# An S5 scan layer on Trainium2: rotating the scan's inputs in place in six chunk slots, with a new instruction order

## The chip, the cores and the metric

The kernel runs on one core of one Trainium2 chip. The time is that of one execution on the device, in microseconds (us), and less is better. Engines are named as the profile names them: PE is TensorE (PEld its weight loads), DVE is VectorE, ACT is ScalarE, POOL is GpSimd, SP is SyncE.

## The reference, cut to what matters

```python
xn = layernorm(x)                                  # x: 1 x 2048 x 1024, bfloat16
# part A: a diagonal complex recurrence over 2048 steps, 1024 states
Bu = einsum("bld,pd->blp", xn, B_bar)              # complex B_bar
for t in range(2048):
    h = Lam_bar * h + Bu[:, t, :]                  # complex Lam_bar
y = 2 * einsum("blp,dp->bld", h_all, C).real + xn * Dskip
# part B: the two tokens with the largest xn @ w_r go through a gated MLP (1024 x 3584)
return x + y + part_B
```

The kernel cuts the 2048 steps into 16 chunks of 128. The scan instruction that it uses on DVE is given a real recurrence. So within each chunk the input is turned by the angle of `Lam_bar` to the power of minus t ("turn in", TI), then two real scans run with the modulus of `Lam_bar` as decay (SC), and their result is turned back ("turn out", TO). One turn of a complex array is three DVE instructions: a product with the cosines, a product of the swapped halves (real and imaginary part exchanged) with the signed sines, and a sum.

## The kernel before

A frame is two chunks. PE computes `Bu` for a frame, one block of 128 states at a time; ACT moves it from PSUM into `u`; DVE turns `u` into `v`; the scan reads `v`. Tables `E1c` and `E1s` hold cosines and signed sines.

```python
def evac_u(f, j):                                  # ACT
    if j == 0:
        u_tiles[f] = work.tile([128, 2, PT, TF], BF16, name="u", bufs=2)
    nc.scalar.copy(out=u_tiles[f][:, :, j, :], in_=pB_tiles.pop((f, j))[:])

def v_tile(c):
    if c not in v_tiles:
        v_tiles[c] = work.tile([128, 2, PT, T + 2], BF16, name="v", bufs=2)
    return v_tiles[c]

def turn_in(c, js=ALLJ):                           # DVE
    f, cc = divmod(c, CPF)
    u = u_tiles[f][:, :, js, cc * T:(cc + 1) * T]
    v = v_tile(c)
    m = work.tile([128, 2, PT, T], BF16, name="m", tag="m")
    rot = v[:, :, js, 2:]
    nc.vector.tensor_tensor(out=rot, in0=u, in1=both(E1c, js), op=ALU.mult)
    nc.vector.tensor_tensor(out=m[:, :, js, :], in0=u[:, ::-1], in1=E1s[:, :, js, :], op=ALU.mult)
    nc.vector.tensor_add(out=rot, in0=rot, in1=m[:, :, js, :])
...
def turn_out(c, js=ALLJ):                          # DVE; cut
    nc.vector.tensor_tensor(out=rot, in0=g, in1=E2c[:, :, js, :], op=ALU.mult)
    nc.vector.tensor_tensor(out=m[:, :, js, :], in0=g[:, ::-1], in1=both(E2s, js), op=ALU.mult)
    nc.vector.tensor_add(out=rot, in0=rot, in1=m[:, :, js, :])
```

`u[:, ::-1]` is the swap. There is one scratch tile `m` for all turns. Chunks 0 to 3 are turned in two halves, the last chunk in three parts, all others whole: 22 turns in and 22 turns out. The order of all instructions comes from a small planner: every task has a duration, its dependencies and a priority, and a table `ADJUST` of searched numbers shifts the priorities.

Of the kernel before, what the change touches and what calls it, by code (L numbers as in the profile page):

```python
# [9 lines left out]
ACT = mybir.ActivationFunctionType  # L10
ALU = mybir.AluOpType
# [6 lines left out]
T = 128  # L18
TF = 256
# [6 lines left out]
    ('x', 4): -5.4, ('x', 6): 45.2, ('x', 8): 30.6, ('x', 9): 9.9, ('x', 10): 81.6, ('x', 11): 60.3, ('x', 12): 21.2,  # L26
    ('B', 5, 0): 1.8, ('B', 5, 1): 1.6, ('B', 6, 0): 2.8, ('B', 6, 1): 38.2, ('B', 7, 0): 42.4, ('B', 7, 1): 15.8,
    ('C', 0, 0): 21.6, ('C', 0, 1): 20.8, ('C', 1, 0): 2.1, ('C', 1, 1): -2.7,
    ('sum', 5): 26.9, ('sum', 10): 38.6, ('sum', 12): 204.6, ('sum', 15): 15.9,
    ('nmr1', 6): 56.1, ('nmr1', 7): 212.5, ('nmr1', 9): 214.1, ('nmr1', 10): 74.8, ('nmr1', 11): 61.1,  # L30
    ('sq', 7): -48.4,
    ('xnT', 7): -3.8434110173345237, ('xnT', 8): 2.330756354758774, ('xnT', 9): -1.9681120886767554,
    ('xnT', 11): -0.20571159998656965, ('xnT', 12): 35.53687818863374, ('xnT', 13): -5.08116404784938,
    ('xnT', 14): -1.6392153513862842, ('xnT', 15): -42.082253982643586,
    ('nmr', 8): -107.7, ('nmr', 10): -98.5,
    ('rstd', 9): 5.9,
    ('sin',): -3.6,
    ('ts', 1, 0): 172.7, ('ts', 1, 1): 108.6,
    ('E2n', 0): 1.2, ('E2n', 1): -21.3,
    ('Bu', 1, 0): -7.9, ('Bu', 1, 1): -5.9, ('Bu', 1, 2): -31.7, ('Bu', 1, 3): -0.8, ('Bu', 1, 4): -5.6,  # L40
    ('Bu', 1, 5): -10.1, ('Bu', 1, 6): -0.2, ('Bu', 4, 0): -22.1, ('Bu', 4, 1): 4.5, ('Bu', 4, 2): -2.5,
    ('Bu', 4, 3): 5.0, ('Bu', 4, 4): -6.4, ('Bu', 4, 5): -2.2, ('Bu', 4, 7): -0.6, ('Bu', 5, 0): 20.6,
    ('Bu', 5, 1): -49.1, ('Bu', 5, 2): 20.5, ('Bu', 5, 3): -0.3, ('Bu', 5, 4): -8.4, ('Bu', 5, 5): -0.7,
    ('Bu', 5, 6): -15.7, ('Bu', 5, 7): -6.8, ('Bu', 6, 0): 51.2, ('Bu', 6, 1): -9.1, ('Bu', 6, 2): 1.9,
    ('Bu', 6, 3): -7.5, ('Bu', 6, 4): -12.6, ('Bu', 6, 5): 2.0, ('Bu', 6, 6): -22.7, ('Bu', 6, 7): 1.9,
    ('Bu', 7, 0): 290.1, ('Bu', 7, 1): -0.4, ('Bu', 7, 2): -0.1, ('Bu', 7, 3): 11.1, ('Bu', 7, 4): -9.4,
    ('Bu', 7, 5): 9.3, ('Bu', 7, 6): 29.7, ('Bu', 7, 7): -1.4,
    ('u', 2, 0): -11.8, ('u', 2, 1): -26.4, ('u', 2, 2): 34.9, ('u', 2, 3): 2.1, ('u', 2, 5): -4.0,
    ('u', 2, 6): -4.9, ('u', 3, 1): -16.1, ('u', 3, 2): -44.1, ('u', 3, 4): -44.6, ('u', 3, 7): 1.0,
    ('u', 4, 0): 15.6, ('u', 4, 1): 44.8, ('u', 4, 2): 42.7, ('u', 4, 4): -3.8, ('u', 4, 5): 11.0, ('u', 4, 6): 7.7,  # L50
    ('u', 4, 7): 17.3,
    ('TI', 0, 0): -19.7, ('TI', 0, 4): -3.0, ('TI', 1, 0): -4.9, ('TI', 1, 4): -7.9, ('TI', 8, 0): 62.9,
    ('TI', 9, 0): 73.1, ('TI', 11, 0): -11.8, ('TI', 13, 0): 30.7, ('TI', 14, 0): -38.5, ('TI', 15, 0): 346.6,
    ('TI', 15, 4): -34.3, ('TI', 15, 6): 673.0,
    ('cw', 0, 0): 12.6, ('cw', 0, 4): 12.6, ('cw', 1, 0): 12.5, ('cw', 1, 4): 13.3,
    ('SC', 1, 0, 0): 22.2, ('SC', 1, 0, 1): 75.7, ('SC', 1, 4, 0): 23.4, ('SC', 1, 4, 1): 3.3,
    ('SC', 3, 0, 0): 112.8, ('SC', 3, 0, 1): 6.5, ('SC', 3, 4, 0): 7.0, ('SC', 3, 4, 1): 10.7, ('SC', 4, 0, 0): -0.1,
    ('SC', 4, 0, 1): -11.3, ('SC', 12, 0, 0): 18.6, ('SC', 12, 0, 1): 3.0, ('SC', 15, 0, 0): 25.5,
    ('SC', 15, 0, 1): 22.6, ('SC', 15, 4, 0): 41.8, ('SC', 15, 4, 1): 22.5, ('SC', 15, 6, 0): 45.9,
    ('SC', 15, 6, 1): 7.2,  # L60
    ('TO', 2, 0): 11.0, ('TO', 2, 4): -7.4, ('TO', 4, 0): -50.9, ('TO', 12, 0): 34.1, ('TO', 13, 0): -130.1,
    ('xr', 0): -17.4, ('xr', 3): 13.0, ('xr', 4): 21.4, ('xr', 5): 34.6, ('xr', 6): 49.5, ('xr', 7): 49.6,
    ('xr', 8): 55.2, ('xr', 9): 56.6, ('xr', 10): 84.8, ('xr', 11): 69.2, ('xr', 12): 93.2, ('xr', 13): 87.9,
    ('xr', 14): 189.0, ('xr', 15): 224.2,
    ('Y', 2, 0): 40.8, ('Y', 2, 1): 0.2, ('Y', 2, 2): 3.9, ('Y', 2, 3): -17.0, ('Y', 3, 0): -23.2, ('Y', 3, 1): 0.3,
    ('Y', 3, 2): 11.7, ('Y', 3, 3): 3.3, ('Y', 6, 0): -4.6, ('Y', 6, 1): 1.7, ('Y', 6, 2): 7.9, ('Y', 6, 3): -8.6,
    ('Y', 10, 0): 18.7, ('Y', 10, 1): 54.9, ('Y', 10, 2): 30.2, ('Y', 10, 3): 5.8, ('Y', 11, 0): 4.6,
    ('Y', 11, 1): 4.6, ('Y', 11, 2): -11.7, ('Y', 11, 3): -0.2, ('Y', 12, 0): 48.7, ('Y', 12, 1): -1.0,
    ('Y', 12, 2): 15.0, ('Y', 12, 3): 18.1,
    ('ADD', 4, 0): 66.6, ('ADD', 4, 1): 8.9,  # L70
    ('xm', 9): 32.0, ('xm', 10): 23.8,
    ('w', 3): -25.8, ('w', 16): 88.5, ('w', 18): 165.2, ('w', 20): 219.3, ('w', 22): 156.0, ('w', 23): 216.5,
    ('w', 24): 167.0, ('w', 25): 222.5, ('w', 26): 167.6, ('w', 27): 179.1, ('w', 28): 168.4, ('w', 29): 222.5,
    ('w', 30): 231.4, ('w', 31): 166.6, ('w', 32): 210.4, ('w', 33): 166.1, ('w', 34): 187.3, ('w', 35): 257.2,
    ('w', 36): 190.5, ('w', 37): 217.1, ('w', 38): 243.4, ('w', 39): 196.1, ('w', 40): 198.1, ('w', 41): 246.5,
    ('mm', 12): 30.3,
    ('gT', 1): 64.4,
# [88 lines left out]
def kernel(  # L166
# [24 lines left out]
    NF = L // TF  # L191
    CPF = TF // 128
# [81 lines left out]
    for tag, n in (("xt", 4), ("xn", 2), ("xnT", NF - 2), ("pT", 1), ("pB", 3), ("pY", 3), ("u", 2), ("v", 2), ("gf", 2),  # L274
                   ("gb", 2), ("hT", 3), ("xr", 1), ("xa", 1), ("ot", 2), ("w", 2)):
        pl.ring(tag, n)
# [47 lines left out]
    xnT_tiles = {}  # L324
# [66 lines left out]

    def xnT_part(c):
        f, cc = divmod(c, CPF)
        if f not in xnT_tiles:
            xnT_tiles[f] = work.tile([128, DT, TF], BF16, name="xnT", bufs=NF - 2)
        return xnT_tiles[f][:, :, cc * T:(cc + 1) * T]
# [43 lines left out]
    for c in range(NCH):  # L440
        ln = c - 30
        xn_out = ("Tpe", c) if c < PE_T else ("T", c)
        xnT_take = ("xnT", c // CPF, [("Y", (c // CPF) * CPF + 1, 2)])
# [29 lines left out]
        if c < PE_T:  # L473
            if c == 0:
                add(("TpeA",), "PE", 0.24, lambda: transpose_half(0), [("applyA",)], key=ln - 10, takes=[("pT", ("T", c), [("xnT", c)])])
                add(("Tpe", c), "PE", 0.24, lambda: transpose_half(1), [("apply", c), ("TpeA",)], key=ln - 10, takes=[("pY", ("T", c), [("xnT0",)])])
                add(("xnT0",), "DVE", 0.42, evac_T0, [("Tpe", c)], key=-36, takes=[xnT_take])
            else:
                add(("Tpe", c), "PE", 0.48, lambda c=c: transpose_pe(c), [("apply", c)], key=ln - 10,
                    takes=[("pY" if c < 4 and c % 2 else "pT", ("T", c), [("xnT", c)])])  # L480
            add(("xnT", c), "ACT", 0.92 if c else 0.55, lambda c=c: evac_T(c), [("Tpe", c) if c else ("TpeA",)], key=-41 + c if c < 2 else ln - 10, takes=[xnT_take])
        else:
            add(("T", c), "SP", 1.35, lambda c=c: transpose_dma(c), [("apply", c)], key=-60 + c, takes=[xnT_take], mb=0.28, lag=0.7)
# [156 lines left out]
    def stage_Bu(f, j, ts_=slice(0, TF)):  # L640
# [3 lines left out]
        for ri in range(2):  # L644
            for k in range(DT):
                nc.tensor.matmul(out=pB[:, ri, ts_], lhsT=BT[ri][j][:, k, :], rhs=xnT_tiles[f][:, k, ts_],  # L646
                                 start=(k == 0), stop=(k == DT - 1))

    def evac_u(f, j):
        if j == 0:  # L650
            u_tiles[f] = work.tile([128, 2, PT, TF], BF16, name="u", bufs=2)
        nc.scalar.copy(out=u_tiles[f][:, :, j, :], in_=pB_tiles.pop((f, j))[:])  # L652

    HALVES = ((0, 0), (0, 1), (1, 0), (1, 1), (1, 2))
# [4 lines left out]
    for f in range(NF):  # L659
        for j in range(PT):  # L660
            hs = (f, j) in HALVES
            if hs:
                add(("Bh", f, j), "PE", 0.93, lambda f=f, j=j: stage_Bu(f, j, slice(0, T)), [("B", j, 0), ("B", j, 1), ("xnT", f * CPF)] + ([] if f else [("xnT0",)]),
                    key=2 * f - 3 + j / 8, takes=[("pB", (f, j), [("u", f, j)])])
            add(("Bu", f, j), "PE", 0.93 if hs else 1.75, lambda f=f, j=j, hs=hs: stage_Bu(f, j, slice(T if hs else 0, TF)),
                [("B", j, 0), ("B", j, 1)] + [("xnT", f * CPF + cc) for cc in range(CPF)] + ([("Bu", f, j - 1)] if j else [])
                + ([("Bh", f, j)] if hs else []), key=2 * f - 3 + j / 8, takes=[("pB", (f, j), [("u", f, j)])])
# [498 lines left out]
```

## Time and profile before

| | before |
|---|---|
| time, median of 3 runs | 265.95 us |
| span of the profiled run | 264.4 us |
| PE busy | 256.5 us, 97% |
| DVE busy | 251.5 us, 95% |
| ACT busy | 158.9 us, 60% |
| one whole product or sum of a turn (128x2048 bf16) | 1.22 us |
| idle DVE from its first statistics to its last turn | 2.53 us |

PE and DVE are both nearly always busy. The last row is the sum of the gaps of 0.05 us and more between the end of one DVE instruction and the start of the next. (The prediction left out gaps under 0.04 us and got 2.9.)

A row of the timeline has a start, a duration, engine, line, operation, output and inputs. This is the turn in of one whole chunk in the kernel before; the columns are start, duration, engine, line, operation, output and inputs:

```profile
69.64 1.22 DVE L697 TENSOR_TENSOR v<-u,E1c 128x2048 bf16<-128x2048 bf16 x1
70.78 1.22 DVE L698 TENSOR_TENSOR m<-u,E1s 128x2048 bf16<-128x2048 bf16 x1
72.04 1.22 DVE L699 TENSOR_TENSOR v<-v,m 128x2048 bf16<-128x2048 bf16 x1
73.19 0.68 DVE L759 TENSOR_TENSOR hT<-gb,E2c 128x1024 bf16<-128x1024 bf16 x1
```

The first product would end at 70.86, yet the second one starts at 70.78, 0.08 us earlier: the two overlap, and the distance is 1.14 us. The second product ends at 72.00, and the sum starts at 72.04, after it: it needs what the second product writes, and the distance is 1.26 us. The instruction behind the sum overlaps again (1.15). So an instruction that depends on the one directly ahead costs about 0.12 us more of DVE's time than one that doesn't, and no duration shows it. I call such a start **held**.

### The profile page before, as it was taken

What the parts mean: (1) busy time and instruction counts of PE and PEld (TensorE: products, weight loads), DVE (VectorE), ACT (ScalarE), POOL (GpSimd) and SP (SyncE); (2) the same over time, 40 slices, a digit from 0 to 9 for tenths busy, and PEclk for the clock granted to TensorE, in tenths of its full rate; (3) what the DMA queues carried; (4) which work ended last, traced back from release to release, by engine and by line L of the source; (5) the groups of instructions that cost most, each with busy time, mean ns of one, the idle gap of its engine ahead of it and who ended that gap; (6) DMA issues with size and microseconds to landing.
All of it is one profiled execution on the core that took longest, in us unless ns stands there. A gap on an engine that the chain in (4) does not pass through costs nothing.

```text
span 264.4 us, 5522 instructions
## 1 busy us (share of the span) xinstructions
PE 256.5 (97%) x2207; PEld 173.2 (66%) x2227; DVE 251.5 (95%) x334; ACT 158.9 (60%) x281; POOL 83.6 (32%) x126
## 2 busy tenths in 40 slices
PE   7799999999999999999999999999999999999994
PEld 7799988774688457456756586455864776644461
DVE  6999999999999999999999999999998999999992
ACT  3799999959699999996524447034551533145110
POOL 4221303563545440731040217115260409011100
PEclk9999999999999999999999999999999999999999
DMA  8999999998541125416111197588967884770411
GB/s 180 188 175 218 171 235 229 248 271 293 153 137 57 47 60 165 138 40 183 58 62 60 35 360 237 187 266 287 296 235 253 289 272 175 269 288 20 117 46 40
DMA packets 66165, 46.51 MB, mean 176 GB/s; under 512 B 45844, under 2 KB 52122, under 8 KB 66140
## 3 DMA queue, kind: packets, MB, share of 16 engines
q1 hardware_dynamic: 65788, 45.82, 63.4%
q8 instruction: 17, 0.28, 0.5%
q0 software_dynamic: 144, 0.27, 0.3%
q10 hardware_dynamic: 208, 0.07, 0.1%
q14 instruction: 8, 0.07, 0.1%
HBM read 30.94 MB, written 4.20 MB: 133 GB/s over the span
## 4 chain that ended last, share of the span: by engine, by line
PE 61%; DVE 28%; issue 3%; SPq 2%; ACT 2%; DMA 2%; DVEq 0%
PE pB L646 34%; PE pY L849 20%; DVE gf L718 9%; DVE ot L863 3%; PE pG L1048 3%; DVE hT L759 3%; DVE m L760 3%; DVE v L699 2%; DVE v L697 2%; DVE m L698 2%; DMA BT<-in_A_B_im_dram 2%; DVE gb L711 2%; SPq L286 2%; PE pD L1088 1%; PE pY L842 1%
## 5 line engine op out<-in xcount | busy, mean ns | idle before, releaser
L646 PE MATMUL pB<-xnT,BT 128*128 128x256 bf16 (+1 forms) x1104 | 117.5, 265 | 1.1 <-DMA BT<-in_A_B_im_dram 1.1
L849 PE MATMUL pY<-CT,hT 128*128 128x512 bf16 (+1 forms) x508 | 114.8, 372 | 1.7 <-issue 0.5
L646 PEld LDWEIGHTS <-BT 128*128 128x128 bf16 x1104 | 99.7, 98 | 16.2 <-issue 3.2
L849 PEld LDWEIGHTS <-hT 128*128 128x128 bf16 x528 | 49.1, 98 | 52.6 <-issue 3.2
L734 POOL TENSOR_TENSOR cw<-gf,tL 128x16 f32<-128x16 f32 (+1 forms) x38 | 35.0, 924 | 136.1 <-DVE gf L718 135.2
L718 DVE TENSOR_TENSOR_SCAN gf<-R,v 128x1040 f32<-128x1040 f32 (+1 forms) x38 | 69.0, 1851 | 0.2
L652 ACT CAST u<-pB 128x512 bf16<-128x512 f32 x64 | 36.5, 580 | 34.8 <-PE pB L646 34.7
L724 ACT CAST gb<-gf 128x1024 bf16<-128x1024 f32 (+1 forms) x38 | 32.4, 862 | 24.6 <-DVE gf L718 24.5
L810 ACT ACTIVATE xa<-xr,nmr_all,rstd_all 128x1024 f32<-128x1024 bf16 x12 | 14.9, 1239 | 21.9 <-DMA xr<-in_A_x_dram 8.1
L699 DVE TENSOR_TENSOR v<-v,m 128x2048 bf16<-128x2048 bf16 (+2 forms) x22 | 20.6, 938 | 0.8
L761 DVE TENSOR_TENSOR hT<-hT,m 128x2048 bf16<-128x2048 bf16 (+2 forms) x22 | 20.5, 934 | 0.8
L759 DVE TENSOR_TENSOR hT<-gb,E2c 128x2048 bf16<-128x2048 bf16 (+2 forms) x22 | 20.5, 930 | 0.2
L697 DVE TENSOR_TENSOR v<-u,E1c 128x2048 bf16<-128x2048 bf16 (+2 forms) x22 | 20.4, 928 | 0.2
L760 DVE TENSOR_TENSOR m<-gb,E2s 128x2048 bf16<-128x2048 bf16 (+2 forms) x22 | 20.5, 930 | 0.0
L698 DVE TENSOR_TENSOR m<-u,E1s 128x2048 bf16<-128x2048 bf16 (+2 forms) x22 | 20.4, 930 | 0.0
L863 DVE TENSOR_TENSOR ot<-pY,xa 128x512 bf16<-128x512 f32 (+1 forms) x25 | 16.0, 656 | 2.4 <-PE pY L852 1.8
L749 POOL CAST v<-cy 128x16 bf16<-128x16 f32 (+1 forms) x19 | 14.1, 744 | 1.4
L349 ACT ACTIVATE xn<-xt,nmean_all 128x1024 bf16<-128x1024 bf16 x12 | 13.8, 1149 | 0.3
L742 POOL TENSOR_TENSOR cy<-cw 128x16 f32<-128x16 f32 (+1 forms) x19 | 12.8, 674 | 1.5
L343 ACT ACTIVATE xn<-xt 128x1024 bf16<-128x1024 bf16 x12 | 12.6, 1054 | 0.0
L374 ACT ACTIVATE xn<-xt,nmr_all,rstd_all 128x1024 bf16<-128x1024 bf16 x10 | 12.4, 1241 | 0.3
L750 POOL TENSOR_TENSOR v<-cy,v 128x16 bf16<-128x16 f32 (+1 forms) x19 | 11.1, 586 | 1.5
(153 smaller groups left out, 186.6 us busy)
## 6 DMA issues: line engine op xcount, KB each, us to landing
wt<-in_B_w_up_dram SPq DMA_DIRECT2D x14, 512.0 KB, 5.1
wt<-in_B_w_gate_dram SPq DMA_DIRECT2D x14, 512.0 KB, 3.8
wt<-in_B_w_down_dram SPq DMA_DIRECT2D x14, 512.0 KB, 3.9
xt<-in_A_x_dram SPq DMA_DIRECT2D x16, 256.0 KB, 3.1
xr<-in_A_x_dram SPq DMA_DIRECT2D x16, 256.0 KB, 2.5
out_dram<-ot SPq DMA_DIRECT2D x31, 128.0 KB, 2.6
Drow<-in_A_Dskip_dram SPq DMA_DIRECT2D x1, 256.0 KB
xnT<-xn SPq DMA_TRANSPOSE x10, 2.8
```

The source lines that it names most:

```text
L646: nc.tensor.matmul(out=pB[:, ri, ts_], lhsT=BT[ri][j][:, k, :], rhs=xnT_tiles[f][:, k, ts_], start=(k == 0), stop=(k == DT - 1))
L652: nc.scalar.copy(out=u_tiles[f][:, :, j, :], in_=pB_tiles.pop((f, j))[:])
L697: nc.vector.tensor_tensor(out=rot, in0=u, in1=both(E1c, js), op=ALU.mult)
L698: nc.vector.tensor_tensor(out=m[:, :, js, :], in0=u[:, ::-1], in1=E1s[:, :, js, :], op=ALU.mult)
L699: nc.vector.tensor_add(out=rot, in0=rot, in1=m[:, :, js, :])
L718: nc.vector.tensor_tensor_scan(out=flat(gf), data0=flat(R[:, js, :]), data1=flat(v[:, ri, js, :]), initial=0.0, op0=ALU.mult, op1=ALU.add)
L724: nc.scalar.copy(out=gb_tiles[c][:, ri, js, :], in_=gf_tiles[c, js.start, ri][:, :, 2:])
L734: nc.gpsimd.tensor_tensor(out=cw_tiles[c, js.start][:, ri, :, 0:n], in0=g.unsqueeze(1).to_broadcast([128, 2, n]), in1=tL[:, ri, :, js], op ...
L759: nc.vector.tensor_tensor(out=rot, in0=g, in1=E2c[:, :, js, :], op=ALU.mult)
L760: nc.vector.tensor_tensor(out=m[:, :, js, :], in0=g[:, ::-1], in1=both(E2s, js), op=ALU.mult)
L849: nc.tensor.matmul(out=pY[:], lhsT=h_tiles[c][:, ri, j, :], rhs=CT[ri][h][:, j, d0:d0 + w], start=first and c in SKIP_DVE and ri == rs[0] ...
L863: nc.vector.tensor_add(out=y_tiles["ot", c][:, d_], in0=y_tiles.pop(("pY", c, dh))[:], in1=y_tiles["xa", c][:, d_])
```

## The change

The intent: keep the scan's inputs in one array of six chunk slots, rotate each in place instead of copying it from `u` to `v`, and so free memory chunk by chunk; the same for the normed x in twelve slots. With the new constraints the instruction order was searched anew, and block 1 of `B` in frame 0 does its real part first for both chunks, because the imaginary part's table lands later. The core of the diff, cut:

```diff
+    u_all = work.tile([128, NSLOT, 2, PT, T + 2], BF16, name="u_all")      # NSLOT = 6
     def evac_u(f, j):
-        nc.scalar.copy(out=u_tiles[f][:, :, j, :], in_=pB_tiles.pop((f, j))[:])
+        nc.scalar.copy(out=u_all[:, u_slots(f), :, j, 2:].rearrange("p c r t -> p r c t"),
+                       in_=pB_tiles.pop((f, j))[:].rearrange("p r (c t) -> p r c t", t=T))
...
     def v_tile(c):
-        ...
+        return u_all[:, c % NSLOT]
     def turn_in(c, js=ALLJ):
-        u = u_tiles[f][:, :, js, cc * T:(cc + 1) * T]
-        rot = v[:, :, js, 2:]
-        nc.vector.tensor_tensor(out=rot, in0=u, in1=both(E1c, js), op=ALU.mult)
+        u = v_tile(c)[:, :, js, 2:]
         nc.vector.tensor_tensor(out=m[:, :, js, :], in0=u[:, ::-1], in1=E1s[:, :, js, :], op=ALU.mult)
-        nc.vector.tensor_add(out=rot, in0=rot, in1=m[:, :, js, :])
+        nc.vector.tensor_tensor(out=u, in0=u, in1=both(E1c, js), op=ALU.mult)
+        nc.vector.tensor_add(out=u, in0=u, in1=m[:, :, js, :])
...
+    RISPLIT = ((0, 1),)        # this block of B: real part of both chunks first, then the imaginary part
...
-ADJUST = { ... }               # the order of the kernel before
+ADJUST = { ... }               # searched anew
```

Of the two products the first one must read both halves of `u` before the second one overwrites them, so the product of the swapped halves now comes first.

## The prediction

> **What bounds the kernel now.** I read the page first: busy times, then the slices, then the chain that ended last. Two engines are near their limit together.
>
> ```profile
> span 264.4 us, 5522 instructions
> PE 256.5 (97%) x2207; PEld 173.2 (66%) x2227; DVE 251.5 (95%) x334; ACT 158.9 (60%) x281; POOL 83.6 (32%) x126
> ...
> PE 61%; DVE 28%; issue 3%; SPq 2%; ACT 2%; DMA 2%; DVEq 0%
> ```
>
> The chain changes between PE and DVE: PE from 13 to 59 us, DVE from 66 to 119, PE to 232, DVE to 258. So neither can be shortened alone. The second question is how much of either engine's time is waiting. I asked for the busy time from DVE's first statistics (3.4) to its last rotation (258.2), and from the first PE work that waits for B to the same end:
>
> ```profile
> core 0: us, PE busy (x) PEld busy (x) DVE busy (x) ACT busy (x) POOL busy (x), PEclk, DMA share, GB/s
> 3.40:258.20 254.80, 251.60 (x2175) 169.96 (x2193) 249.00 (x323) 157.91 (x281) 81.68 (x115) 1.00 0.66 180
> 13.10:258.00 244.90, 243.25 (x2053) 162.41 (x2073) 239.42 (x298) 152.18 (x266) 79.04 (x105) 1.00 0.64 179
> ```
>
> From 3.4 to 258.2 DVE is idle in some 5.8 us by this sum; walking DVE's timeline with gaps under 0.04 us left out, only 2.9 us remain, the rest being the small steps between instructions. PE's own idle after 13.1 is 1.65 us. These are all the waiting that a better order has to win. The lines that carry the waits:
>
> ```profile
> 13.12 0.62 PE L646 MATMUL pB<-xnT,BT 128*128 128x128 bf16 x8 [1.13 <-DMA BT<-in_A_B_im_dram]
> ...
> DVE ot L863 <- PE pY L852: 1.8, 2, 1.5
> ...
> DVE guT L1077 <- PE pU L1068: 0.7, 1, 0.7
> ...
> DVE ot L863 <- PE pY L849: 0.5, 1, 0.5
> ...
> DVE row L918 <- PE pR L914: 0.4, 1, 0.4
> ```
>
> The first is PE at the start, waiting for the second B table; the second is the tail after the last rotation, which no buffer shortens; the other three, 0.67 + 0.52 + 0.44 = 1.63 us, are DVE waiting in the middle for PE results that the order placed a little late.
>
> **What the Trainium skill says.** (1) "Perfetto Trace Analysis", Identifying the Most-Contended Engine: matmul busy share is no good measure of headroom, because matmuls are pipelined. So I checked the pace: in the chain, 16 Y matmuls of 512 columns take 3.45 us, 216 ns each, and 32 Bu matmuls of 256 take 3.49, 109 ns each. (2) "TensorE: Matmul & The Clock Gate", "Wait — 56ns, not 53.3ns?", gives columns over 2.4 GHz plus about 2.5 ns, 215.7 ns for 512 columns; the trace agrees, so PE streams at its limit and its 97% is real here. (3) "VectorE: DVE Perf Modes", Mode 2×_1P, wants 16-bit data, step ±1 and 4-byte alignment. The new slots have rows of 130 elements (260 bytes), started at element 2 (4 bytes): aligned. The old v has just this layout, and the trace shows no cost in it, as the rows below show. (4) The first-named PE page, Architectural detail, says that VectorE's queue is strict FIFO: a late rT then holds up all DVE work behind it, whatever buffers are free. The 0.44 us before the copy from pR is such a wait.
>
> ```profile
> L761 DVE TENSOR_TENSOR hT<-hT,m 128x2048 bf16<-128x2048 bf16 x11 | 13.5, 1225 | 0.4
> L699 DVE TENSOR_TENSOR v<-v,m 128x2048 bf16<-128x2048 bf16 x11 | 13.5, 1224 | 0.4
> L697 DVE TENSOR_TENSOR v<-u,E1c 128x2048 bf16<-128x2048 bf16 x11 | 13.4, 1220 | 0.1
> L652 ACT CAST u<-pB 128x512 bf16<-128x512 f32 x64 | 36.5, 580 | 34.8 <-PE pB L646 34.7
> ```
>
> **The change, part by part.**
>
> In-place rotation. u (two frames of two chunks, 16 KB a partition) and v (two chunks, 8.1 KB) become six slots of 2 x 8 x 130 x 2 bytes, 24.4 KB: the same memory. The instruction count does not change: DVE has 333 rows before and after, ACT 264, POOL 131. The three rotation multiplies and adds stay, only the product from the swapped halves comes first. L699 is already in place and takes 1224 ns against 1225 for rows without padding, so cost 0. ACT writes u in four rows of 128 instead of two of 256; I allow 0 to 50 ns on 580, times 64 = up to 3 us, on an engine busy 60% of the span: no direct cost.
>
> Buffer waits. A wait for a u or v buffer shows nowhere in the list of waits (ACT's 34.7 us before u is for PE, with pB). So freed slots remove no wait by themselves; they only allow another order: now TI of chunks 2 and 3 stands before SC of chunk 1, and frame 3's PE work could run earlier. The twelve xn slots likewise: same 24 KB, freed a chunk at a time.
>
> Start. In Bu(0,1) the two orders differ in work: instead of both parts of B on chunk 0, then on chunk 1 (32 matmuls of 128 columns), PE does the real part on both chunks (8 of 256) and then the imaginary part (8 of 256). Before, PE did 8 of 128, waited to 13.12, and still had 8 + 16 of 128 to do: 24 x 56.6 ns = 1.36 us. After, 8 x 109 ns = 0.88 remain when the same table lands. Gain 1.36 - 0.88 = **0.48 us**, if the transposes of chunks 1 and 2 stay in the waiting time, as the order has them. PE loses 16 rows of weights and 16 of matmuls in this way.
>
> The new order. To see what it does I added up the trace's durations along each engine's order (TI or TO 3.54 us for a full chunk, 1.92 for a half; a full scan 2.24, half 1.17; ADD 0.585; a frame's Bu 1.77; a quarter of Y 1.735; the skip products 0.25), anchored DVE at 3.39 and PE at its start of Bu(0,1). On the kernel before these sums meet the trace within 1 us (Y(2,0) 85.1 against 85.03; scan of chunk 4 89.4 against 88.40). For the changed order they say:
> - ADDs come later after their Y: smallest distance 1.0 us where it was 0.2 (chunk 6). The 0.52 and 0.67 us waits should go: **-1.2 us on DVE**.
> - Y of chunk 3 now stands right behind Y(2,0), at 87.2 - 0.5 = 86.7 on PE, but its rotation ends on DVE at 89.4, less the 1.0 bias 88.4: PE waits for some **1.7 us** in all at the first four chunks.
> - rT sits behind Bu(4,6), at 128.6 - 0.5 + 1.7 = 129.8; DVE gets to the copy at 128.7 - 0.8 = 127.9. DVE waits **up to 1.9 us**, where it waited 0.44.
>
> Sum for PE: -0.5 + 1.7, less about 0.6 of small waits seen now = +0.6. Sum for DVE: -1.2 + 1.9 - 0.4 = +0.3. Without the two new waits it would be -0.5 - 0.6 = -1.1 on PE and -1.6 on DVE. Each wait is a difference of two long sums with about 1 us of error, and the order was searched anew for this layout, which speaks for waits smaller than mine. I take the middle of +0.6 and about -1.6, that is **-0.55 us: 265.4**.
>
> **Rivals.**
> 1. The order wins all waits and the head start: DVE then loses 1.63 and PE 0.5 + 0.6. The end needs both, so about -1.5 us, 264.4. For it: wider ADD distances. Against: the rT sum.
> 2. The new waits are real and push PE for good, since PE has no idle time later to catch up in: +0.6 to +1.5, 266.5 to 267.4.
> 3. ACT becomes the bound between 60 and 120 us. It is busy 19.55 of 20 us from 100 to 120, holds the norm's passes and now the strided evacuations. 32 evacuations x 50 ns would add 1.6 us there, and late norm rows would delay r(14) and rT: +1 us. Against: the same elements, in rows still long.
> 4. DVE's in-place reads are slower. At 70 ns per operation and some 16 chunks that is 1.1 us straight onto the time. Against: L699's 1224 ns.
>
> **Range and chances.** A 2% gain is 5.3 us; all waits that DVE has between 3.4 and 258.2 are 2.9, and no work is removed, so faster by over 2% is all but excluded: 0.02. A loss of 5.3 us would take several rivals at once: 0.03. Range 263.7 to 267.1: rival 1 with something to spare below, rival 2 above.
>
> **What the profile will show.** DVE busy within 1.5 us of 251.5 and the rotation rows at 1.22 us (else rival 4); the u evacuation near 580 ns (else rival 3); PE's first wait for B gone or shorter; a wait of DVE for pR of about 1 to 2 us near 128; a PE wait for hT near 87 us; no more waits of ADD and guT. The prediction is wrong if DVE's work itself changes, or if a wait over 2 us appears that my sums did not see, most likely on ACT's rows.

## The result, and the profile after

| | before, same rounds | after |
|---|---|---|
| time, median | 266.1 us (265.9 to 266.69, 4 runs) | 269.04 us (268.95 to 269.77, 4 runs) |
| span of the profiled run | 264.4 us | 267.1 us |
| DVE busy | 251.5 us | 253.1 us |
| idle DVE up to its last turn | 2.53 us | 2.82 us |
| end of DVE's last turn | 258.20 us | 260.96 us |

The ratio is 1.0113, with a 95% interval of 1.0089 to 1.0137. A ratio here is always the mean time of one kernel's fast runs over that of the kernel before in the same rounds, so it is not quite the ratio of the medians quoted beside it. The changed kernel is about 3 us slower (within 2%), where the prediction had it 0.55 us faster.

The page of the kernel after, its busy times and the chain that ended last:

```profile
span 267.1 us, 5499 instructions
...
PE 256.5 (96%) x2191; PEld 172.8 (65%) x2211; DVE 253.1 (95%) x334; ACT 159.2 (60%) x281; POOL 83.0 (31%) x126
...
DVE 46%; PE 37%; ACT 7%; issue 5%; DMA 4%; SPq 0%; DVEq 0%; ACTq 0%
```

PE has the same busy time, but the chain has moved: DVE holds 46% of it instead of 28%, PE 37% instead of 61%. DVE is busy 1.6 us longer with the same 334 instructions. Which of them became slower? The groups of the turn in, and the evacuation (busy us, then mean ns of one, then idle us just before):

```profile
L718 DVE TENSOR_TENSOR u_all<-u_all,E1c 128x2048 bf16<-128x2048 bf16 x11 | 13.5, 1226 | 0.4
L719 DVE TENSOR_TENSOR u_all<-u_all,m 128x2048 bf16<-128x2048 bf16 x11 | 13.5, 1225 | 0.4
...
L717 DVE TENSOR_TENSOR m<-u_all,E1s 128x2048 bf16<-128x2048 bf16 x11 | 13.3, 1212 | 0.2
```

None of them: 1212 to 1226 ns, and 1220 to 1225 before. The durations of all 334 instructions add up to 269.0 us in both kernels. Busy time counts a stretch in which two instructions overlap only once, so the 1.6 us are overlap that was lost. The last column is a trace of the answer: two rows of a turn in have 0.4 us ahead of them, where before only the sum had (0.4, against 0.1 and 0.0 for the products). The row of the second product before, which the prediction doesn't show:

```profile
L698 DVE TENSOR_TENSOR m<-u,E1s 128x2048 bf16<-128x2048 bf16 x11 | 13.5, 1225 | 0.0
```

The timeline of one turn in shows what this means:

```profile
64.63 1.23 DVE L717 TENSOR_TENSOR m<-u_all,E1s 128x2048 bf16<-128x2048 bf16 x1
65.89 1.23 DVE L718 TENSOR_TENSOR u_all<-u_all,E1c 128x2048 bf16<-128x2048 bf16 x1
67.15 1.22 DVE L719 TENSOR_TENSOR u_all<-u_all,m 128x2048 bf16<-128x2048 bf16 x1
```

Both distances are 1.26 us. The second product now writes what the first one reads, so it is held, and it no longer overlaps the first. In the compiled program all 22 second products of a turn in wait on DVE's own semaphore for the first; before, 10 of the 22 had no wait at all and the other 12 waited for something older. So what costs goes with a wait for the instruction directly ahead; no run has the dependency without the wait, so which of the two costs is not separated.

To see what this is worth in all, I added up the distances from start to start on DVE, by kind, from the first statistics to the end of the last turn (us; gaps of 0.05 us and more are counted apart, as idle). The same sums for the experiments follow in the same table, so that it need not be shown again:

```
                      ends at   TI products   TI sum   TO products   TO sum   scans   idle
before                 258.20      39.83       19.11      39.90       18.79   72.78   2.53
after                  260.96      42.34       19.15      39.85       19.40   72.45   2.82
x1_before_inplace      260.56      42.39       19.43      39.87       19.34   72.12   2.06
x2_before_mfirst       258.30      39.77       19.43      39.90       19.36   72.19   2.34
x3_after_const         259.56      39.78       19.19      39.80       19.49   72.43   3.60
x4_after_oldorder      261.34      42.38       19.50      39.89       19.35   72.11   2.97
x5_before_split        258.79      39.83       19.21      39.84       18.83   72.77   3.22
x8_after_sep           260.58      40.76       19.23      38.68       19.42   72.79   4.87
x9_before_split_sep    259.06      39.39       19.26      38.56       18.66   73.08   5.14
y2_after_const         258.57      39.73       19.21      39.78       19.45   72.45   2.96
y4_oldorder_const      258.90      39.66       19.57      39.86       19.40   72.10   3.22
```

The two products of the turns in took 39.83 us before and 42.34 after: +2.51 us, and DVE's last turn ends 2.76 us later. Worked out from the distances of single instructions it is nearly the same: for whole chunks the median distance went from 1.14 to 1.25 us, for halves from 0.60 to 0.72, so 11 x 0.11 + 9 x 0.12 = 2.3 us, and two quarter parts besides.

The waits moved too. These are waits of the kernel after (who waited for whom: total us, times, longest):

```profile
PE pB L659 <- ACT u_all L667: 2.4, 4, 0.9
DVE hT L779 <- ACT gb L744: 2.1, 2, 1.6
...
PEld L931 <- DVE r_bf L927: 0.7, 1, 0.7
```

The second is new, and it is on DVE. Its longer part, in DVE's timeline:

```profile
116.51 4.53 DVE L738 TENSOR_TENSOR_SCAN gf<-R,u_all 128x1040 f32<-128x1040 f32 x2
122.65 1.23 DVE L779 TENSOR_TENSOR hT<-gb,E2c 128x2048 bf16<-128x2048 bf16 x1 [1.61 <-ACT gb L744]
```

Two scans run to about 121.0, and the turn out that stands right behind them in the new order needs ACT to cast their results. ACT is in the middle of a norm pass then:

```profile
120.44 1.14 ACT L360 ACTIVATE xn<-xt,nmean_all 128x1024 bf16<-128x1024 bf16 x1
...
121.59 1.03 ACT L744 CAST gb<-gf 128x1024 bf16<-128x1024 f32 x1
```

The cast starts at 121.59, and DVE stands idle for 1.61 us. With a second wait of the same kind (0.53 us at 113) this makes 2.14 us of new waiting, against the 1.63 us of old waits (for pY, pU and pR) that are gone. So idle DVE is nearly what it was, 2.82 against 2.53, and the waits don't explain the 3 us; the held starts are the candidate.

### The profile page after: what moved, and what is told of

The parts are those of the page before. It is cut to its first block, busy times and chain, and to the rows that moved or that the text cites. A ratio compares the mean times of both kernels' runs of the same rounds, so it can differ in the third digit from the quotient of the medians.

```text
span 267.1 us, 5499 instructions
## 1 busy us (share of the span) xinstructions
PE 256.5 (96%) x2191; PEld 172.8 (65%) x2211; DVE 253.1 (95%) x334; ACT 159.2 (60%) x281; POOL 83.0 (31%) x126
## 4 chain that ended last, share of the span: by engine, by line
DVE 46%; PE 37%; ACT 7%; issue 5%; DMA 4%; SPq 0%; DVEq 0%; ACTq 0%
PE pB L659 17%; PE pY L866 15%; DVE gf L738 11%; DVE u_all L718 4%; DVE m L717 4%; DVE u_all L719 3%; DVE hT L779 3%; DVE m L780 3%; DVE hT L781 3%; DMA wt<-in_B_w_up_dram 3%; PE pG L1065 3%; DVE ot L880 2%; DVE gb L731 2%; DVE st L345 2%; ACT xn L360 1%
## 5 line engine op out<-in xcount | busy, mean ns | idle before, releaser
L659 PE MATMUL pB<-xnT_all,BT 128*128 128x256 bf16 (+1 forms) x1088 | 117.5, 266 | 2.4 <-ACT u_all L667 2.4
L754 POOL TENSOR_TENSOR cw<-gf,tL 128x16 f32<-128x16 f32 (+1 forms) x38 | 35.6, 937 | 138.3 <-DVE gf L738 137.5
L738 DVE TENSOR_TENSOR_SCAN gf<-R,u_all 128x1040 f32<-128x1040 f32 (+1 forms) x38 | 69.2, 1854 | 0.1
L667 ACT CAST u_all<-pB 128x512 bf16<-128x512 f32 x64 | 36.2, 580 | 28.4 <-PE pB L659 28.3
L718 DVE TENSOR_TENSOR u_all<-u_all,E1c 128x2048 bf16<-128x2048 bf16 (+2 forms) x22 | 20.6, 935 | 0.8
L719 DVE TENSOR_TENSOR u_all<-u_all,m 128x2048 bf16<-128x2048 bf16 (+2 forms) x22 | 20.6, 934 | 0.8
L717 DVE TENSOR_TENSOR m<-u_all,E1s 128x2048 bf16<-128x2048 bf16 (+2 forms) x22 | 20.3, 922 | 0.4
L769 POOL CAST u_all<-cy 128x16 bf16<-128x16 f32 (+1 forms) x19 | 14.6, 767 | 1.2
L762 POOL TENSOR_TENSOR cy<-cw 128x16 f32<-128x16 f32 (+1 forms) x19 | 10.9, 575 | 1.5
L770 POOL TENSOR_TENSOR u_all<-cy,u_all 128x16 bf16<-128x16 f32 (+1 forms) x19 | 10.9, 572 | 1.5
```

The lines of the kernel that those rows point to most:

```text
L659: nc.tensor.matmul(out=pB[:, ri, ts_], lhsT=BT[ri][j][:, k, :], rhs=xnT_all[:, k, x0 + ts_.start:x0 + ts_.stop], start=(k == 0), stop=(k = ...
L667: nc.scalar.copy(out=u_all[:, u_slots(f), :, j, 2:].rearrange("p c r t -> p r c t"), in_=pB_tiles.pop((f, j))[:].rearrange("p r (c t) -> p ...
L718: nc.vector.tensor_tensor(out=u, in0=u, in1=both(E1c, js), op=ALU.mult)
L719: nc.vector.tensor_add(out=u, in0=u, in1=m[:, :, js, :])
L738: nc.vector.tensor_tensor_scan(out=flat(gf), data0=flat(R[:, js, :]), data1=flat(v[:, ri, js, :]), initial=0.0, op0=ALU.mult, op1=ALU.add)
L754: nc.gpsimd.tensor_tensor(out=cw_tiles[c, js.start][:, ri, :, 0:n], in0=g.unsqueeze(1).to_broadcast([128, 2, n]), in1=tL[:, ri, :, js], op ...
```

## The experiments

Eleven kernels were run in three batches, each five rounds, each batch on one chip beside the kernel before. Two theories stood against each other at the start. **Hold:** the in-place product costs some 2.5 us on DVE through held starts, whatever the order. **Order:** the newly searched order is worse on the chip than the old one, through the waits for ACT.

### The in-place turn alone, put into the kernel before

```diff
-    nc.vector.tensor_tensor(out=rot, in0=u, in1=both(E1c, js), op=ALU.mult)
     nc.vector.tensor_tensor(out=m[:, :, js, :], in0=u[:, ::-1], in1=E1s[:, :, js, :], op=ALU.mult)
-    nc.vector.tensor_add(out=rot, in0=rot, in1=m[:, :, js, :])
+    nc.vector.tensor_tensor(out=u, in0=u, in1=both(E1c, js), op=ALU.mult)
+    nc.vector.tensor_add(out=rot, in0=u, in1=m[:, :, js, :])
```

> The kernel before, its order and buffers untouched; only the first rotation's products are swapped and the second of them is written over u itself (m from the swapped halves, then u times cosine into u, then the sum into v), as the changed kernel does. Theory of the held multiply (in place, the second product must wait until the first has read u, and a held DVE instruction starts 0.11 us later): 22 rotations x 0.11 = 2.5 us, plus some 8 rotations that now start with a write to m right behind a sum that read it, 0.9 us: time +2.5 to +3.4 us over the kernel before. Theory of the order (the new order and ACT's late evacuations cost the 2.9 us): no change, within 0.5 us.

It took 268.3 us (268.12 to 268.81) where the kernel before took 266.37, ratio 1.0067 (1.0033 to 1.0100), with a right result. By the medians that is 1.9 us, less than was expected. (The run of 268.79 us among those of the kernel before lowers the ratio.) Some of the loss was hidden: the wait for pU, 0.67 us in the kernel before, is gone here, since DVE comes later. In DVE's timeline the second product starts behind the first one's end, as it does in the changed kernel:

```profile
70.73 1.20 DVE L697 TENSOR_TENSOR m<-u,E1s 128x2048 bf16<-128x2048 bf16 x1
71.96 1.22 DVE L698 TENSOR_TENSOR u<-u,E1c 128x2048 bf16<-128x2048 bf16 x1
73.22 1.22 DVE L699 TENSOR_TENSOR v<-u,m 128x2048 bf16<-128x2048 bf16 x1
```

So the edit alone, with the old order, the old buffers and the old layout, carries the longer products of the table (42.39 us).

### The new order of the products, but nothing in place

```diff
-    nc.vector.tensor_tensor(out=rot, in0=u, in1=both(E1c, js), op=ALU.mult)
     nc.vector.tensor_tensor(out=m[:, :, js, :], in0=u[:, ::-1], in1=E1s[:, :, js, :], op=ALU.mult)
+    nc.vector.tensor_tensor(out=rot, in0=u, in1=both(E1c, js), op=ALU.mult)
     nc.vector.tensor_add(out=rot, in0=rot, in1=m[:, :, js, :])
```

> Control of the former: the kernel before with the two products swapped (m first), but nothing in place: u is only read, v is written second. Held-multiply theory: only the write to m right behind a sum that read m is held, some 8 times 0.11 = +0.9 us at most; start to start of the first two products stays at 1.14. Order theory: 0.

It took 266.82 us (266.31 to 267.18), ratio 1.0012 (0.9979 to 1.0045): not told apart from the kernel before. The difference to the run above is only whether the second product writes over its input, and the second product overlaps the first again:

```profile
69.49 1.20 DVE L697 TENSOR_TENSOR m<-u,E1s 128x2048 bf16<-128x2048 bf16 x1
70.61 1.23 DVE L698 TENSOR_TENSOR v<-u,E1c 128x2048 bf16<-128x2048 bf16 x1
71.87 1.23 DVE L699 TENSOR_TENSOR v<-v,m 128x2048 bf16<-128x2048 bf16 x1
```

The distance is 1.12 us instead of 1.23, and the medians of the two kernels differ by 268.3 - 266.82 = 1.5 us. The table has a small thing besides: the sums of the turns take 38.79 us here and 37.90 before. My reading is that `m` is now written by the first instruction of a turn in, and where that stands directly behind the sum of another turn, which reads the same `m`, this start is held as well. The traces bear it out: it stands so eight times, and it starts 0.73 us behind a sum of 128x1024 where it was 0.61, and 1.33 us behind one of 128x2048 where it was 1.14. The eight come to 1.1 us on DVE. What they are worth in time isn't resolved.

### The changed kernel without the hold, and with the old order

The first edit lets the first product of a turn in read a table instead of `u`. It has the same size and type, but nothing that the second product overwrites, so no hold is needed. (Where the first product had to wait for ACT to fill `u`, the second does so instead.) The result is wrong (relative error 0.073). The second edit leaves the changed kernel's code and forces every engine's tasks into the order of the kernel before.

```diff
-    ...tensor_tensor(out=m[:, :, js, :], in0=u[:, ::-1], in1=E1s[:, :, js, :], op=ALU.mult)
+    ...tensor_tensor(out=m[:, :, js, :], in0=both(E1c, js), in1=E1s[:, :, js, :], op=ALU.mult)   # wrong on purpose
```

```diff
-    pl.run().emit()
+    pl.run()
+    pl.order = FORCED          # the list of tasks as the kernel before has them
+    pl.emit()
```

> The changed kernel with the first product reading a constant table of the same shape instead of u (the result is wrong on purpose), so the in-place product has nothing of it to wait for. Same instructions, same order. Held-multiply theory: the second product starts 1.14 us behind the first instead of 1.25, 22 x 0.11 = 2.46 us less on DVE; of it up to 1.2 us may be lost again at the wait for ACT near 122 us: time -1.3 to -2.5 us under the changed kernel (266.5 to 267.7). Order theory: no change from 269.0.

> The changed kernel (slots, in-place rotation, split of Bu(0,1)) with every engine's tasks in the order of the kernel before. Held-multiply theory: the order is not what costs, so +2.5 to +3.4 us over the kernel before, like the first run. Order theory: about the time of the kernel before, within 0.5 us.

Without the hold the changed kernel took 267.23 us (266.6 to 268.16), ratio 1.0023 (0.9986 to 1.0059). With the old order it took 269.49 us (268.86 to 269.88), ratio 1.0104 (1.0069 to 1.0138): no better than with its own order. In the run without the hold the products overlap again:

```profile
64.70 1.22 DVE L717 TENSOR_TENSOR m<-E1c,E1s 128x2048 bf16<-128x2048 bf16 x1
65.84 1.22 DVE L718 TENSOR_TENSOR u_all<-u_all,E1c 128x2048 bf16<-128x2048 bf16 x1
67.09 1.23 DVE L719 TENSOR_TENSOR u_all<-u_all,m 128x2048 bf16<-128x2048 bf16 x1
```

The distance is 1.14 us, and the products' sum in the table is back at 39.78. The second product still writes in place. So it isn't the in-place writing itself that costs, but that the instruction directly ahead reads the old values.

### Both causes crossed, on one chip

The runs above had come beside each other in one batch with the kernel before, but the changed kernel itself was not in it. The four combinations were therefore run together: held or not, new order or old. The edits are the same as above, alone or together.

> The changed kernel again, so that four kernels stand side by side on one chip: two orders, each with the second product held and not held. Both theories: 269.0, +2.9 us over the kernel before.

> New order, not held (the first product reads a constant; wrong on purpose). Held-multiply theory: 1.5 to 2.2 us under the changed kernel, and within 0.5 to 1.2 us of the kernel before. Order theory: as the changed kernel.

> Old order, held: slots and in-place rotation in the order of the kernel before. Held-multiply theory: within 0.7 us of the changed kernel (269 to 269.7). Order theory: as the kernel before, 266.1.

> Old order, not held (wrong on purpose). Held-multiply theory: 1.5 to 2.5 us under the former and within 1 us of the kernel before; then the difference between the orders is under 0.7 us held or not. Order theory: as the former.

| median us (ratio to the kernel before, at 266.17) | new order | old order |
|---|---|---|
| held | 269.36 (1.0118) | 269.03 (1.0099) |
| not held (wrong) | 267.46 (1.0044) | 267.04 (1.0034) |

Read down a column: the hold costs 269.36 - 267.46 = 1.90 us in the new order and 269.03 - 267.04 = 1.99 us in the old one. In this batch no run that is held came in as low as any that isn't (268.19 is the lowest of the one kind, 268.14 the highest of the other). Read along a row: the new order costs 0.3 to 0.4 us, but the runs of the two orders overlap, so this isn't resolved. The order theory falls as the main cause, and the hold stands: two thirds of the 3 us.

The last third is not settled. The kernel without a hold and with the old order is still 0.9 us behind the kernel before (1.0034, interval 1.0008 to 1.0060). What is left in it are the slots, their layout, a buffer less for the carries (`cw`), the product order and the real part first in block 1. The product order alone gave +0.45 us in its run, which was not resolved, and longer sums on DVE, which this kernel has too (38.97 against 37.90 us in the table). Its trace also has two waits for ACT's cast, 0.39 and 1.13 us, that the kernel before lacks; the head start below brings the same two. These are places where time goes in the trace; no experiment takes them away.

The clean counter-test would be the changed kernel with a second scratch tile, into which one of the products goes, so that it gives the right result with nothing written over. It did not fit: with the second tile in place, the weights' pool needs 16 KB in each partition and 12 are left, so the build failed and there was no run.

### The head start on PE alone

```diff
-    def stage_Bu(f, j, ts_=slice(0, TF)):
+    def stage_Bu(f, j, ts_=slice(0, TF), ris=(0, 1)):
-        for ri in range(2):
+        for ri in ris:
...
+    # block (0, 1): Bh does ris=(0,), both chunks; Bu does ris=(1,), both chunks; order otherwise as before
```

> The kernel before with one thing of the change alone: the first frame's second block of Bu is computed real part first for both chunks, then the imaginary part, so that PE has work while the second B table is on its way. My prediction counted 0.48 us for this. If DVE alone sets the time (it is busy from 3.4 us on), PE's head start is worth nothing: 0, within 0.3 us. If PE counts as much as DVE, -0.4 to -1.2 us.

It took 266.87 us (265.67 to 267.26) beside 266.05, ratio 1.0020 (0.9995 to 1.0045). The half microsecond that PE wins at the start is worth nothing at the end. The trace adds something: instruction by instruction, DVE is 0.45 us ahead of the kernel before from 25 to 109 us, and 0.59 us behind from 125 us on. In between stand two waits for ACT's cast that the kernel before doesn't have, 0.27 us and this one:

```profile
120.70 1.22 DVE L870 TENSOR_TENSOR hT<-gb,E2c 128x2048 bf16<-128x2048 bf16 x1 [1.13 <-ACT gb L835]
```

ACT was late because it had waited 1.29 us for rows of x from a DMA; why these came late is open. All runs of the changed code in the old order have this pair too (0.33 to 0.43 us, and 1.13), so it is not the new order alone that makes DVE wait for ACT. In the changed kernel PE had the same head start and more: it does the second half of this block at 11.84 us, where the kernel before was still waiting until 13.12.

### Can the held starts be bought back?

If a start is held only because the instruction directly ahead is the one it depends on, another instruction between the two should free it. I put an independent scan, small product or sum of the skip path between the second product and the sum of a turn, in 25 turns of the changed kernel, and in 16 turns of the kernel before (with the head start of the last run).

```diff
-    ('TI', 5, 0), ('ADD', 0, 1),
+    ('TI', 5, 0, 'products'), ('ADD', 0, 1), ('TI', 5, 0, 'sum'),        # and so on
```

> The changed kernel, correct, with its order but for one shift: in the 25 rotations that are followed on DVE by an independent scan, add or small product, that instruction is put between the second product and the sum, so the sum is no longer held by the instruction just ahead of it. Held-instruction theory: 25 x 0.11 = -2.7 us on DVE if the waits for other engines stay; up to half of it may be lost to waits: -1.3 to -2.7 us under the changed kernel (266.3 to 267.7). If holding costs nothing in itself: no change, or slower, since an instruction comes earlier than its data.

> The kernel before with the split of the first frame and with the same shift in its 16 rotations that have an independent successor: -16 x 0.11 = -1.8 us on DVE. PE is nearly as full (1.65 us idle after 13 us), so the gain is capped by the head start of PE and its idle time: -0.5 to -1.5 us under the kernel before (264.6 to 265.6). A version that beats both if it holds.

Both missed. The changed kernel so treated took 268.94 us, ratio 1.0104 (1.0082 to 1.0125); the kernel before 267.39, ratio 1.0046 (1.0025 to 1.0067), slower than without the two edits; beside the head start alone (1.0020) the intervals overlap. The mechanism did work. In the first of the two, with an addition of the skip path in between, the next start comes 1.14 us behind the second product, and the sum follows 0.60 us behind the start of the addition:

```profile
65.81 1.22 DVE L843 TENSOR_TENSOR u_all<-u_all,E1c 128x2048 bf16<-128x2048 bf16 x1
66.95 0.68 DVE L1009 TENSOR_TENSOR ot<-pY,xa 128x512 bf16<-128x512 f32 x1
67.55 1.22 DVE L845 TENSOR_TENSOR u_all<-u_all,m 128x2048 bf16<-128x2048 bf16 x1
```

In the table the products took 2.75 us less than in the changed kernel (40.76 + 38.68 against 42.34 + 39.85). But DVE waited 2.05 us more (4.87 against 2.82), probably because the instructions pulled forward were not always ready, and the turns' own results came later. Two waits that the changed kernel didn't have (its two for ACT's cast are here as well, 0.53 and 1.70 us):

```profile
131.03 0.21 DVE L1064 COPY row<-pR 16x128 bf16<-16x128 bf16 x1 [0.57 <-PE pR L1060]
...
172.92 0.69 DVE L1009 TENSOR_TENSOR ot<-pY,xa 128x512 bf16<-128x512 f32 x1 [0.55 <-PE pY L995]
```

A searched order that knows the price of a held start might keep some of the 2.7 us; I didn't make one, and no version tried here beats the kernel before.

## Why the prediction was right or wrong, point by point

- **"L699 is already in place and takes 1224 ns against 1225 for rows without padding, so cost 0": this is the step that failed.** The duration was right (1226 ns after the change) and was the wrong thing to look at. The cost lies in the distance of starts. L699 depends on the instruction directly ahead already, so its start is always held; the change added a second held start per turn in, 22 in all. They measured +2.51 us in DVE's sums and 1.9 to 2.0 us of time. The sign was in the lines that the prediction showed: L699 and L761 with 0.4 us of idle time ahead of them, L697 with 0.1. And a timeline of any turn would have shown 1.14 us to the second product against 1.26 to the sum. The prediction's own sums held it too: its 3.54 us for a full turn are less than three durations of 1.22 us, and they were kept for the changed kernel, where the three distances are 1.25, 1.26 and 1.14, 3.65 us.
- **Rival 4, in-place reads slower, at 70 ns each for some 16 chunks, 1.1 us "straight onto the time".** This rival had the right place, and the right reason why little of it is hidden, but not the mechanism: the reads are not slower. It was rejected with the same durations, and it was too small besides: it is 0.11 to 0.12 us for 22 starts.
- **The evacuation of u at 0 to 50 ns more.** It was 580 ns before and after:

```profile
L667 ACT CAST u_all<-pB 128x512 bf16<-128x512 f32 x64 | 36.2, 580 | 28.4 <-PE pB L659 28.3
```

- **Freed slots remove no wait by themselves.** Nothing speaks against it: idle DVE went from 2.53 to 2.82 us, and to 2.97 with the slots in the old order.
- **The start, 0.48 us won on PE.** PE's wait for the second B table did go, but the gain has no worth: the kernel before with this part alone was not faster (1.0020).
- **The waits of ADD and guT go, 1.2 us.** Right in the trace, but in part by luck: guT's wait is also gone in the first experiment, which keeps the old order and only makes DVE later. And it was paid back: 2.14 us of waits for ACT's cast came in. The prediction named ACT's crowded stretch from 100 to 120 us (rival 3), but expected the victim to be the copy from pR.
- **A new DVE wait for pR of up to 1.9 us, and 1.7 us of PE waiting for hT near 87.** Neither came. DVE itself was late for pR, so PE and its weights waited 0.7 us for DVE there; PE's larger waits were for ACT's evacuation, 2.4 us in four pieces. These were differences of two long sums, and my sums did not contain DVE's own slowing.
- **DVE busy within 1.5 us of 251.5.** It was 253.1, off by 1.6. The prediction said itself that it would be wrong if DVE's work changed; it changed without a change in any duration.
- **Slips that change nothing.** The page counts 334 instructions on DVE, 281 on ACT and 126 on POOL, not 333, 264 and 131, and the middle of +0.6 and -1.6 is -0.5, not -0.55.

## What to carry to other kernels

On an engine that is the bound, count the distance from start to start, not the duration: an in-place write right behind an instruction that reads the old values turns two overlapping instructions into two in a row. Before an edit that saves memory in this way, ask which instruction stands directly ahead, and whether it touches the same tile. Instructions put between to undo this must be ready at that moment, or the gain comes back as a wait.

## What the Trainium skill lacked or had wrong

- "VectorE: DVE Perf Modes", The DRAIN you can't avoid, says that a semaphore between DVE instructions "costs nothing extra here", measured with copies. In this case's traces a wait for the instruction directly ahead does cost: a product of 128x2048 bf16 starts 1.25 us (median) behind the last one if it has to wait for it, and 1.14 us if not; for 128x1024 it is 0.72 against 0.60 us. Eleven whole and nine half turns of this made 2.3 of the 2.5 us more in DVE's sums.
- The same page, Two Vector instructions with no wait between them, says that a held instruction starts only when every earlier Vector instruction has finished. The traces agree for the case of a wait: the held product starts at 65.89 us, after 64.63 + 1.23 = 65.86, and the one that isn't held 0.08 us ahead of the other's end (70.78 against 70.86). But that section gives no size for the loss, and its rule for what is held speaks of quadrants. "Perfetto Trace Analysis" knows an overlap with the next instruction, but does not say that a wait gives it up; no page says that writing over the input of the instruction directly ahead is also paid for, 0.11 to 0.12 us each time.
- No page says that another instruction between the two takes the cost away. Here it did: the addition put between a second product and its sum started 1.14 us behind the product, where the sum itself starts 1.26 us behind it, and over 25 turns the products took 2.75 us less.
